# Key-value products in two 64-column halves of the array, and the masks moved to GpSimd

## The chip, the cores and the metric

The kernel runs on one core of one Trainium2 chip. The metric is the device time of one execution in microseconds (us). The profile is of one execution on that core; its span is the time from the first to the last instruction of the program.

The engines are named as the profile names them: PE is TensorE (PEld its weight loads), DVE is VectorE, ACT is ScalarE, POOL is GpSimd, SP is SyncE, which issues most DMAs.

## The reference

The input x has 2048 rows of 512 features. It is normalised per row; the result xn feeds two branches, and the output is x plus both.

```python
def _A_ref(x, wqkv, w_phi, wo):                      # H = 32 heads of 16
    q, k, v = ...                                    # from x @ wqkv
    pq = jnp.einsum("bhsd,hdf->bhsf", q, w_phi)
    pk = jnp.einsum("bhsd,hdf->bhsf", k, w_phi)
    phi_q = concatenate([softmax(pq), softmax(-pq)])
    phi_k = concatenate([softmax(pk), softmax(-pk)])
    kv = jnp.einsum("bhsf,bhsd->bhfd", phi_k, v)
    z  = jnp.einsum("bhsf->bhf", phi_k)
    num = jnp.einsum("bhqf,bhfd->bhqd", phi_q, kv)
    den = jnp.einsum("bhqf,bhf->bhq", phi_q, z) + 1e-6
    return (num / den) @ wo
def _B_ref(x, w1, b1, w2):                           # 512 -> 1792 -> 512
    h = x @ w1 + b1
    return (h * tanh(softplus(h))) @ w2
```

So the first branch is a linear attention: for each of the 32 heads the keys' features (16 from the softmax, 16 from the softmax of the negative) are multiplied with the head's 16 values and summed over all 2048 rows, and the queries' features are then multiplied with that small matrix. Features and values of different heads never meet.

## The kernel before, in words

The 2048 rows are 16 tiles of 128, in 4 groups of 4 tiles. The projection of q and k is folded with w_phi into the weights wqp and wkp.

The first half of the program goes through slots s = 0 to 3 in a loop. In slot s it does, in program order: the exponentials of the keys' logits of group s on ACT (`exponentials`, L228); the products of the features and values of group s - 1 on PE (`accumulate`, L282); two value projections copied by DVE, the logits of the next group and two more value projections copied by ACT (`value`, L164; `logits`, L194; the matmuls are L156); the statistics and normalisation of x two groups ahead (`ln_stats`, and `ln_apply`, L128, on POOL in slots 0 and 1); the division of the features by their sums on DVE (`normalise`, L246 to L259); a number of blocks of the second branch (`hidden`, matmuls L176, activation L183); and the extremes of the next group on DVE (`extremes`, L207 to L218). In slot 2 the transposed q weights are loaded and folded. Each engine runs its instructions in the order in which the program issues them.

After the loop come the exponentials of the first queries, `accumulate(3)`, `mask_kv`, more logits, and then the second half: `attend` (L326) multiplies transposed features of the queries (qT, transposed by DMA that SP issues, L237) with the masked matrix, ACT copies the result out (L335 to L342), `combine` on DVE divides, a DMA transposes (L386), and `project_out` (L408) adds the output projection to the second branch's sum (`second_layer`, L399). `residual` adds x and sends the tile out.

The parts that the change touches:

- `vext` (L81): two buffers with the values of one group, for each tile 4 blocks j of 128 values followed by 8 columns of ones (136 per block). A block holds 8 heads. `value` writes 128 values per block in one copy; the ones are written once at the start by POOL (L443).
- `accumulate(g)`: for each of the 4 blocks, both signs of the softmax (pl) and the 4 tiles of the group, one matmul. Its stationary operand is 128 features (8 heads of 16), its moving operand the 128 values of the same block and one column of ones: 129 columns. It adds up in PSUM over all 16 tiles; `blocks` (L263) gives the place, 432 columns of three banks at a pitch of 144. The result is 128 x 128 for each block, of which only the 8 squares of 16 x 16 on the diagonal mean anything, and a column of sums.
- `mask_kv` (L291): DVE multiplies the 128 x 128 part by a mask with ones in the 8 squares (KVmask, L293 and L297), and spreads the column of sums over 8 columns, masked as well (L303, L308). It writes `kvm`, whose blocks have 144 columns: 128 values, 8 sums, 8 columns of a plain mask.
- `KVmask` and the last 8 columns of `kvm` are written once at the start by three DVE copies (L444 to L446) from `block`, which POOL makes.

Of the kernel before, what the change touches and what calls it, by code (L numbers as in the profile page):

```python
# [8 lines left out]
BF16 = mybir.dt.bfloat16  # L9
# [3 lines left out]
ALU = mybir.AluOpType  # L13
# [4 lines left out]
def kernel(  # L18
# [12 lines left out]
    nc = tc.nc  # L31
    P = 128
    S, D, NH, DH, F = 2048, 512, 32, 16, 1792
    NG = 4
    TPG = 4
# [21 lines left out]
    vpool = ctx.enter_context(tc.tile_pool(name="vpool", bufs=1))  # L57
# [7 lines left out]
    kvm = persist.tile([P, 2, 4, 144], BF16, name="kvm")  # L65
# [12 lines left out]
    mhalf = consts.tile([P, TPG], FP32, name="mhalf")  # L78
    block = consts.tile([P, 8, 16], BF16, name="block")
    KVmask = consts.tile([P, 136], FP32, name="KVmask")  # L80
    vext = [vpool.tile([P, TPG, 4, 136], BF16, name=f"vext{i}") for i in range(2)]  # L81

    ctx.enter_context(tc.manual_schedule())

# [2 lines left out]
    def load_turned(base_col):  # L87

        wT = lnp.tile([P, 4, 512], BF16, name="wT", tag="xn")
        nc.sync.dma_start_transpose(out=wT[:], in_=A_wqkv[:, base_col : base_col + D])  # L90
        return wT

    def fold(wT, dst, dve):

        for kt in range(KT):
            pf = ps.tile([P, 512], FP32, name="pfold", tag="mm")
            for j in range(4):
                nc.tensor.matmul(
                    pf[:, j * P : (j + 1) * P],
                    lhsT=wT[:, j, kt * P : (kt + 1) * P],  # L100
                    rhs=Wbd[:, j, :],
                    start=True,
                    stop=True,
                )
            if kt in dve:
                nc.vector.tensor_copy(dst[:, kt, :], pf[:])
            else:
                nc.scalar.copy(dst[:, kt, :], pf[:])

    def ln_stats(t0, n):  # L110

        stats = lnp.tile([P, TPG, nc.vector.BN_STATS_DIM], FP32, name="stats")
        mv = lnp.tile([P, TPG, nc.vector.BN_AGGR_DIM], FP32, name="mv")
        rstd = lnp.tile([P, TPG], FP32, name="rstd")
        for i in range(n):
            nc.vector.bn_stats(stats[:, i, :], x_sb[:, t0 + i, :])  # L116
        for i in range(n):
            nc.vector.bn_aggr(mv[:, i, :], stats[:, i, :])
        nc.gpsimd.tensor_scalar(
            out=rstd[:, 0:n], in0=mv[:, 0:n, 1], scalar1=1e-5, scalar2=None, op0=ALU.add  # L120
        )
        nc.gpsimd.tensor_tensor(out=rstd[:, 0:n], in0=rstd[:, 0:n], in1=mhalf[:, 0:n], op=ALU.pow)
        return mv, rstd
# [27 lines left out]
    def project(w, t, pp=None):  # L151

        if pp is None:
            pp = ps.tile([P, 512], FP32, name="pproj", tag="mm")[:]
        for kt in range(KT):
            nc.tensor.matmul(  # L156
                pp, lhsT=xnT[:, t, kt, :], rhs=w[:, kt, :],
                start=(kt == 0), stop=(kt == KT - 1),
            )
        return pp  # L160

    def value(t, copy):
        pv = project(wv, t)
        copy(  # L164
            vext[(t // TPG) % 2][:, t % TPG, :, 0:128], pv.rearrange("p (j c) -> p j c", j=4)
        )

    units = iter([(g, f) for g in range(NG) for f in range(FT)])
# [21 lines left out]
    def logits(s, i, copy):  # L190
        if i == 0:
            p_of[s] = smx.tile([P, TPG, 512], BF16, name="p_sb", bufs=1)
        pp = project(wkp if s < NG else wqp, (s % NG) * TPG + i)
        copy(p_of[s][:, i, :], pp)  # L194
# [30 lines left out]
    def exponentials(s, ks=(0, 1)):  # L225
        for k in ks:
            v = e_of[s][:, 2 * k : 2 * k + 2, :, :]
            nc.scalar.activation(v, v, ACT.Exp)  # L228
            if s >= NG:
                turn(s, k)  # L230
# [32 lines left out]
    def blocks(kv, pl, j, width):  # L263

        bank, at = (pl, j) if j < 3 else (2, pl)
        return kv[:, bank, at * 144 : at * 144 + width]

    def by_parts(kv, c0, c1):

        v = kv[:, :, 0:432].rearrange("p b (k c) -> p b k c", c=144)  # L270
        return v[:, 0:2, :, c0:c1], v[:, 2, 0:2, c0:c1]

    kv_of = {}

    def accumulate(g):
        if g == 0:
            kv_of[0] = ps2.tile([P, 3, 512], FP32, name="pkv", tag="kv")
        e = e_of.pop(g)
        for j in range(4):
            for pl in range(2):  # L280
                for i in range(TPG):
                    nc.tensor.matmul(  # L282
                        blocks(kv_of[0], pl, j, 129),
                        lhsT=e[:, i, pl, j * P : (j + 1) * P],
                        rhs=vext[g % 2][:, i, j, 0:129],
                        start=(g == 0 and i == 0 and (j == 0 or (j == 3 and pl == 0))),
                        stop=(g == NG - 1 and i == TPG - 1),
                        skip_group_check=True,
                    )

    def mask_kv():  # L291
        a, b = by_parts(kv_of[0], 0, 128)
        nc.vector.tensor_tensor(  # L293
            out=kvm[:, :, 0:3, 0:128], in0=a,
            in1=KVmask[:, None, None, 0:128].to_broadcast([P, 2, 3, 128]), op=ALU.mult,
        )
        nc.vector.tensor_tensor(  # L297
            out=kvm[:, :, 3, 0:128], in0=b,
            in1=KVmask[:, None, 0:128].to_broadcast([P, 2, 128]), op=ALU.mult,
        )  # L300
        a, b = by_parts(kv_of[0], 128, 129)
        for pl in range(2):
            nc.vector.scalar_tensor_tensor(  # L303
                out=kvm[:, pl, 0:3, 128:136], in0=a[:, pl].to_broadcast([P, 3, 8]), scalar=5e-7,
                in1=KVmask[:, None, 128:136].to_broadcast([P, 3, 8]),
                op0=ALU.add, op1=ALU.mult,
            )
        nc.vector.scalar_tensor_tensor(  # L308
            out=kvm[:, :, 3, 128:136], in0=b.to_broadcast([P, 2, 8]), scalar=5e-7,
            in1=KVmask[:, None, 128:136].to_broadcast([P, 2, 8]), op0=ALU.add, op1=ALU.mult,  # L310
        )

    nd_of, oT_of, po_of, tmp_of = {}, {}, {}, {}
# [121 lines left out]
    for sign in (1, -1):  # L435
        nc.gpsimd.affine_select(
            out=block[:], in_=block[:], pattern=[[-16 * sign, 8], [0, 16]],
# [2 lines left out]
        )  # L440
    nc.gpsimd.memset(mhalf[:], -0.5)
    for i in range(2):
        nc.gpsimd.memset(vext[i][:, :, :, 128:136], 1.0)  # L443
    nc.vector.tensor_copy(KVmask[:, 0:P], block[:].rearrange("p h d -> p (h d)"))  # L444
    nc.vector.tensor_copy(KVmask[:, P : P + 8], block[:, :, 0])
    nc.vector.tensor_copy(  # L446
        kvm[:].rearrange("p l j c -> p (l j) c")[:, :, 136:144],
        block[:, None, :, 0].to_broadcast([P, 8, 8]),
    )


    dve, act = nc.vector.tensor_copy, nc.scalar.copy

    warm = ps.tile([P, 4, P], FP32, name="warm", tag="mm")
    for _ in range(12):
        nc.tensor.matmul(
            warm[:], lhsT=ident[:], rhs=ident[:, None, :].to_broadcast([P, 4, P]),
            start=True, stop=True,
# [4 lines left out]
        out=Wbd[:].rearrange("p j (h e) -> p j h e", h=8),  # L463
        in0=block[:, None, :, :].to_broadcast([P, 4, 8, 16]),
        in1=wsrc[:, :, None, :].to_broadcast([P, 4, 8, 16]),
        op=ALU.mult,
# [17 lines left out]
    def normal(t0, st, xn):  # L484
        ln_apply(t0, TPG, *st, xn, 0)
        for i in (0, 2):
            ln_turn_dma(t0 + i, xn, i)
# [6 lines left out]
    for i in range(TPG):  # L494
        value(i, act)
    hidden(5)

    for s in range(NG):
        exponentials(s, (0, 1) if s else (0,))
        if s > 0:  # L500
            accumulate(s - 1)
        if s < NG:
            for i in range(2 if s else 0):
                value(s * TPG + i, dve)
        if s == 0:
            p_of[1] = smx.tile([P, TPG, 512], BF16, name="p_sb", bufs=1)
            act(p_of[1][:, 0, :], project(wkp, TPG))
            exponentials(0, (1,))
            wide = ps2.tile([P, 3, 512], FP32, name="pwide", tag="kv")
            for i in range(3):  # L510
                project(wkp, TPG + 1 + i, wide[:, i, :])
        else:
            for i in range(TPG):
                logits(s + 1, i, act)
        if 0 < s < NG:
            for i in range(2, TPG):
                value(s * TPG + i, act)
        ln = s + 2 < NG
        if ln:
            t0 = (s + 2) * TPG  # L520
            st = ln_stats(t0, TPG)
            xn = lnp.tile([P, TPG, D], BF16, name="xn", tag="xn")
        elif s == 2:
            wT = load_turned(0)

        normalise(s, 0, (lambda: normal(t0, st, xn)) if ln else None)
        normalise(s, 1)
        if s == 2:
            fold(wT, wqp, ())
        if s == 0:  # L530
            hidden(6)
            act(p_of[1][:, 1:4, :], wide[:])
        hidden((11, 14, 8, 10)[s])
        extremes(s + 1)
# [21 lines left out]
    for h in range(2 * NG):  # L556
        t = 2 * h + 4
# [55 lines left out]
```

## Time and profile before

| what | value |
|---|---|
| median of 3 runs | 183.64 us (183.57 to 183.75) |
| the profiled execution | 183.6 us |
| its span | 181.9 us |
| instructions | 2744 |
| PE matmuls, busy | 1024 records, 175.4 us |
| PE weight loads, busy | 1039 records, 90.2 us |
| DVE, ACT, POOL busy | 146.5, 126.5, 25.0 us |
| granted PE clock | 1.00 |
| DMA | 18.02 MB, 99 GB/s on average |

How to read it: the profiled execution's own time is 1.7 us more than its span, which is what lies around the program. A busy time is the union of an engine's records. Matmul records overlap and their ends are modelled, so the price of a matmul in a stream is the distance between two starts and not the length of a record. In a chain of waits each piece is what the next one waited for; only what lies on it moves the end.

### The profile page before, as it was taken

How to read it: one execution, taken by the hardware profiler on the slowest of the kernel's cores; microseconds unless marked ns; L12 is line 12 of the kernel's file. 1: busy time of each engine (PE TensorE's matmuls, PEld its weight loads, DVE VectorE, ACT ScalarE, POOL GpSimd, SP SyncE). 2: the span in 40 equal slices, each digit the busy share in tenths (PEclk: the TensorE clock that was granted, in tenths of full speed). 3: DMA queues.
4: the chain of work that ended last, by engine and by line, in shares of the span. 5: the costliest groups of instructions: out<-in, count | busy, mean ns of one | idle time of the engine just before them, and what ended most of it. 6: DMA issues, size and time to landing. Idle time of an engine off the chain costs nothing.

```text
span 181.9 us, 2744 instructions
## 1 busy us (share of the span) xinstructions
PE 175.4 (96%) x1024; PEld 90.2 (50%) x1039; DVE 146.5 (81%) x255; ACT 126.5 (70%) x194; POOL 25.0 (14%) x30
## 2 busy tenths in 40 slices
PE   6899999999999999999999999999999999999993
PEld 2454344465444645564465555455554545455561
DVE  2989979986999899988999786399916997647963
ACT  2367999999898899979986989472842558235300
POOL 4403079300793000000000000000000000000000
PEclk9999999999999999999999999999999999999999
DMA  6997796300023600000000840963079302990633
GB/s 145 291 401 267 160 356 175 60 0 5 0 50 65 119 0 0 0 0 4 0 0 0 153 81 10 189 147 63 0 171 203 88 5 41 200 192 31 76 101 115
DMA packets 44393, 18.02 MB, mean 99 GB/s; under 512 B 36828, under 2 KB 43868, under 8 KB 44380
## 3 DMA queue, kind: packets, MB, share of 16 engines
q1 hardware_dynamic: 43408, 17.50, 40.6%
q10 hardware_dynamic: 972, 0.35, 0.7%
q8 instruction: 8, 0.13, 0.3%
q14 instruction: 5, 0.04, 0.1%
HBM read 6.84 MB, written 2.10 MB: 49 GB/s over the span
## 4 chain that ended last, share of the span: by engine, by line
PE 78%; DVE 11%; ACT 4%; DMA 4%; issue 1%; DVEq 0%
PE po L399 22%; PE ph L176 22%; PE pproj L156 17%; PE po L408 7%; PE pkv L282 4%; PE pnd L326 4%; DVE stats L116 4%; ACT e L228 2%; DMA ob<-ob 2%; DMA x_sb<-in_A_x_dram 2%; DVE m L207 2%; DVE xn L128 1%; ACT L183 1%; DVE e L218 1%; DVE wkp L376 1%
## 5 line engine op out<-in xcount | busy, mean ns | idle before, releaser
L399 PE MATMUL po<-w_sb,acts 128*128 128x512 bf16 (+1 forms) x232 | 50.4, 366 | 0.3
L176 PE MATMUL ph<-xnT,w_sb 128*128 128x512 bf16 x224 | 49.5, 379 | 0.4 <-ACT acts L183 0.4
L183 ACT ACTIVATE acts<-ph,b1f 128x512 bf16<-128x512 f32 x56 | 35.2, 703 | 2.8 <-PE ph L176 2.6
L176 PEld LDWEIGHTS <-w_sb 128*128 128x128 bf16 x224 | 21.9, 98 | 26.7 <-issue 0.6
L228 ACT ACTIVATE e<-e 128x2048 bf16<-128x2048 bf16 x16 | 29.8, 1903 | 6.4 <-DVE e L218 6.3
L399 PEld LDWEIGHTS <-acts 128*128 128x128 bf16 x238 | 22.8, 98 | 22.0
L156 PEld LDWEIGHTS <-xnT 128*128 128x128 bf16 x192 | 18.3, 98 | 21.6 <-DMA xnT<-xn 0.8
L194 ACT CAST p_sb<-pproj 128x512 bf16<-128x512 f32 x25 | 13.7, 587 | 9.4 <-PE pproj L156 9.4
L416 DVE TENSOR_TENSOR x_sb<-po,x_sb 128x512 bf16<-128x512 f32 (+1 forms) x17 | 10.6, 655 | 11.4 <-PE po L408 11.4
L246 DVE TENSOR_REDUCE s<-e 128x128 f32<-128x2048 bf16 x8 | 18.2, 2278 | 1.9 <-ACT e L228 1.9
L128 POOL TENSOR_SCALAR xn<-x_sb,mv,rstd 128x512 bf16<-128x512 bf16 x8 | 16.7, 2100 | 0.2
L408 PE MATMUL po<-wqk,ob 128*128 128x512 bf16 (+1 forms) x66 | 14.7, 366 | 0.3 <-DMA ob<-ob 0.2
L156 PE MATMUL pproj<-wv,xnT 128*128 128x512 bf16 x61 | 14.8, 379 | 0.2
L156 PE MATMUL pproj<-wqk,xnT 128*128 128x512 bf16 x62 | 14.4, 379 | 0.1
L335 ACT CAST wkp<-pnd 128x768 bf16<-128x768 f32 x8 | 6.4, 798 | 11.3 <-PE pnd L326 7.4
L207 DVE TENSOR_TENSOR m<-m 128x512 bf16<-128x512 bf16 (+1 forms) x32 | 11.5, 359 | 1.1
L156 PE MATMUL pproj<-wkp,xnT 128*128 128x512 bf16 x50 | 11.8, 379 | 0.1
L207 DVE TENSOR_TENSOR m<-p_sb 128x1024 bf16<-128x1024 bf16 x16 | 11.0, 685 | 1.0 <-ACT p_sb L194 1.0
L326 PEld LDWEIGHTS <-qT 128*128 128x128 bf16 x128 | 9.1, 98 | 3.8
L116 DVE BATCH_NORM_STATS2 stats<-x_sb 128x6 f32<-128x512 bf16 x16 | 10.0, 679 | 1.2 <-DMA x_sb<-in_A_x_dram 1.2
L326 PE MATMUL pnd<-kvm,qT 128*128 128x144 bf16 x128 | 10.6, 226 | 0.0
L259 DVE TENSOR_TENSOR e<-e,r 128x2048 bf16<-128x2048 bf16 x8 | 10.3, 1281 | 0.3
(67 smaller groups left out, 175.2 us busy)
## 6 DMA issues: line engine op xcount, KB each, us to landing
w_sb<-in_B_w_dram SPq DMA_DIRECT2D x2, 1792.0 KB, 8.9
out_dram<-x_sb SPq DMA_DIRECT2D x15, 128.0 KB, 1.9
x_sb<-in_A_x_dram SPq DMA_DIRECT2D x1, 1024.0 KB, 11.7
x_sb<-in_A_x_dram SPq DMA_DIRECT2D x1, 512.0 KB, 4.0
wv<-in_A_wqkv_dram SPq DMA_DIRECT2D x1, 512.0 KB, 4.8
wqk<-in_A_wo_dram SPq DMA_DIRECT2D x1, 512.0 KB
x_sb<-in_A_x_dram SPq DMA_DIRECT2D x1, 256.0 KB, 3.2
x_sb<-in_A_x_dram ACTq DMA_DIRECT2D x1, 256.0 KB, 3.6
```

Source lines behind the costliest of these rows:

```text
L116: nc.vector.bn_stats(stats[:, i, :], x_sb[:, t0 + i, :])
L128: engine.tensor_scalar(out=xn[:, at + i, :], in0=x_sb[:, t0 + i, :], scalar1=mv[:, i, 0:1], scalar2=rstd[:, i : i + 1], op0=ALU.subtract, ...
L156: nc.tensor.matmul(pp, lhsT=xnT[:, t, kt, :], rhs=w[:, kt, :], start=(kt == 0), stop=(kt == KT - 1),)
L176: nc.tensor.matmul(ph[:], lhsT=w1_sb[:, kt, f * P : (f + 1) * P], rhs=xnT[:, g * TPG : (g + 1) * TPG, kt, :], start=(kt == 0), stop=(kt == ...
L183: nc.scalar.activation(acts[:, f, g * 512 : (g + 1) * 512], ph[:], ACT.Mish, bias=b1f[:, f : f + 1])
L194: copy(p_of[s][:, i, :], pp)
L207: nc.vector.tensor_tensor(out=m[:], in0=src[:, :, 0:half], in1=src[:, :, half : 2 * half], op=op)
L228: nc.scalar.activation(v, v, ACT.Exp)
L246: nc.vector.reduce_sum(t[:], v.rearrange("p t l (c e) -> p (t l c) e", e=16), axis=AX.X)
L326: nc.tensor.matmul(blocks(pnd, pl, j, 144), lhsT=qT_of[h][:, i, pl * 4 + j, :], rhs=kvm[:, pl, j, :], start=True, stop=True,)
L399: nc.tensor.matmul(po[:, c], lhsT=acts[:, f, t * P : (t + 1) * P], rhs=w2_sb[:, f, c], start=(f == 0), stop=False,)
L408: nc.tensor.matmul(po[:, c], lhsT=oT_of[h][:, t % 2 * 4 + j, :], rhs=wo_sb[:, j, c], start=False, stop=(j == 3),)
```

## The change

The 128 features of a block are treated as two halves of 64 (4 heads each). `vext` gets, for each half, its own 64 values and 4 columns of ones (68 per half). `accumulate` issues two matmuls where it issued one: half r takes 64 columns of features, the 64 values of the same half and one column of ones, and writes PSUM partitions 64 r to 64 r + 63. `tile_position=(0, 64 * r)` places it in the left or the right 64 columns of the array, with all 128 rows. The squares off the diagonal between the two halves are no longer computed, so `kvm` is filled with zeros once.

`mask_kv` masks each half of the partitions by itself, in two products of 2 x 3 x 64 and 2 x 64 elements per partition. The new function `masks` writes the zeros, `KVmask` and the last columns of `kvm` on POOL; it is called in slot 2 of the loop, behind the load of the transposed weights, and the three DVE copies at the start are gone.

```diff
--- before.py
+++ after.py
@@ -78,7 +78,7 @@
     mhalf = consts.tile([P, TPG], FP32, name="mhalf")
     block = consts.tile([P, 8, 16], BF16, name="block")
     KVmask = consts.tile([P, 136], FP32, name="KVmask")
-    vext = [vpool.tile([P, TPG, 4, 136], BF16, name=f"vext{i}") for i in range(2)]
+    vext = [vpool.tile([P, TPG, 4, 2, 68], BF16, name=f"vext{i}") for i in range(2)]
 
     ctx.enter_context(tc.manual_schedule())
 
@@ -162,7 +162,8 @@
     def value(t, copy):
         pv = project(wv, t)
         copy(
-            vext[(t // TPG) % 2][:, t % TPG, :, 0:128], pv.rearrange("p (j c) -> p j c", j=4)
+            vext[(t // TPG) % 2][:, t % TPG, :, :, 0:64].rearrange("p j r c -> p (j r) c"),
+            pv.rearrange("p (j c) -> p j c", j=8),
         )
 
     units = iter([(g, f) for g in range(NG) for f in range(FT)])
@@ -279,26 +280,31 @@
         for j in range(4):
             for pl in range(2):
                 for i in range(TPG):
-                    nc.tensor.matmul(
-                        blocks(kv_of[0], pl, j, 129),
-                        lhsT=e[:, i, pl, j * P : (j + 1) * P],
-                        rhs=vext[g % 2][:, i, j, 0:129],
-                        start=(g == 0 and i == 0 and (j == 0 or (j == 3 and pl == 0))),
-                        stop=(g == NG - 1 and i == TPG - 1),
-                        skip_group_check=True,
-                    )
+                    for r in range(2):
+                        c = j * P + 64 * r
+                        nc.tensor.matmul(
+                            blocks(kv_of[0], pl, j, 65)[64 * r : 64 * r + 64],
+                            lhsT=e[:, i, pl, c : c + 64],
+                            rhs=vext[g % 2][:, i, j, r, 0:65],
+                            start=(g == 0 and i == 0 and (j == 0 or (j == 3 and pl == 0))),
+                            stop=(g == NG - 1 and i == TPG - 1),
+                            skip_group_check=True,
+                            tile_position=(0, 64 * r),
+                        )
 
     def mask_kv():
-        a, b = by_parts(kv_of[0], 0, 128)
-        nc.vector.tensor_tensor(
-            out=kvm[:, :, 0:3, 0:128], in0=a,
-            in1=KVmask[:, None, None, 0:128].to_broadcast([P, 2, 3, 128]), op=ALU.mult,
-        )
-        nc.vector.tensor_tensor(
-            out=kvm[:, :, 3, 0:128], in0=b,
-            in1=KVmask[:, None, 0:128].to_broadcast([P, 2, 128]), op=ALU.mult,
-        )
-        a, b = by_parts(kv_of[0], 128, 129)
+        for r in range(2):
+            rows, c = slice(64 * r, 64 * r + 64), slice(64 * r, 64 * r + 64)
+            a, b = by_parts(kv_of[0], 0, 64)
+            nc.vector.tensor_tensor(
+                out=kvm[rows, :, 0:3, c], in0=a[rows],
+                in1=KVmask[rows, None, None, c].to_broadcast([64, 2, 3, 64]), op=ALU.mult,
+            )
+            nc.vector.tensor_tensor(
+                out=kvm[rows, :, 3, c], in0=b[rows],
+                in1=KVmask[rows, None, c].to_broadcast([64, 2, 64]), op=ALU.mult,
+            )
+        a, b = by_parts(kv_of[0], 64, 65)
         for pl in range(2):
             nc.vector.scalar_tensor_tensor(
                 out=kvm[:, pl, 0:3, 128:136], in0=a[:, pl].to_broadcast([P, 3, 8]), scalar=5e-7,
@@ -308,6 +314,15 @@
         nc.vector.scalar_tensor_tensor(
             out=kvm[:, :, 3, 128:136], in0=b.to_broadcast([P, 2, 8]), scalar=5e-7,
             in1=KVmask[:, None, 128:136].to_broadcast([P, 2, 8]), op0=ALU.add, op1=ALU.mult,
+        )
+
+    def masks():
+        nc.gpsimd.memset(kvm[:], 0.0)
+        nc.gpsimd.tensor_copy(KVmask[:, 0:P], block[:].rearrange("p h d -> p (h d)"))
+        nc.gpsimd.tensor_copy(KVmask[:, P : P + 8], block[:, :, 0])
+        nc.gpsimd.tensor_copy(
+            kvm[:].rearrange("p l j c -> p (l j) c")[:, :, 136:144],
+            block[:, None, :, 0].to_broadcast([P, 8, 8]),
         )
 
     nd_of, oT_of, po_of, tmp_of = {}, {}, {}, {}
@@ -440,15 +455,7 @@
         )
     nc.gpsimd.memset(mhalf[:], -0.5)
     for i in range(2):
-        nc.gpsimd.memset(vext[i][:, :, :, 128:136], 1.0)
-    nc.vector.tensor_copy(KVmask[:, 0:P], block[:].rearrange("p h d -> p (h d)"))
-    nc.vector.tensor_copy(KVmask[:, P : P + 8], block[:, :, 0])
-    nc.vector.tensor_copy(
-        kvm[:].rearrange("p l j c -> p (l j) c")[:, :, 136:144],
-        block[:, None, :, 0].to_broadcast([P, 8, 8]),
-    )
-
-
+        nc.gpsimd.memset(vext[i][:, :, :, :, 64:68], 1.0)
     dve, act = nc.vector.tensor_copy, nc.scalar.copy
 
     warm = ps.tile([P, 4, P], FP32, name="warm", tag="mm")
@@ -522,6 +529,7 @@
             xn = lnp.tile([P, TPG, D], BF16, name="xn", tag="xn")
         elif s == 2:
             wT = load_turned(0)
+            masks()
 
         normalise(s, 0, (lambda: normal(t0, st, xn)) if ln else None)
         normalise(s, 1)
```

## The prediction

> **What bounds the kernel now.** I read the page first: shares of the engines, then the chain of work that ended last. After that I read that chain in order of time, the groups of instructions by shape, and the table by stretch for the line that the change rewrites.
>
> ```profile
> PE 175.4 (96%) x1024; PEld 90.2 (50%) x1039; DVE 146.5 (81%) x255; ACT 126.5 (70%) x194; POOL 25.0 (14%) x30
> ...
> PE 78%; DVE 11%; ACT 4%; DMA 4%; issue 1%; DVEq 0%
> ```
>
> TensorE (PE) is busy for 96% of the span, and 78% of the chain is PE work. In order of time the chain lies on PE without a break worth naming from 29.07 us to 106.5 us, and again from 115.5 us to 177.9 us. The line that is rewritten, L282 in `accumulate`, runs four times, and each time it is a piece of that chain:
>
> ```profile
> L282 PE MATMUL pkv<-vext,e 128*128 128x129 bf16 x128 | 7.9, 220 | 0.0
> ...
> L282 PEld LDWEIGHTS <-e 128*128 128x128 bf16 x128 | 7.6, 98 | 0.9
> ```
>
> ```profile
> 39.43:41.24 1.81, 1.81 (x32) 1.80 (x31) 1.00 0.03 9
> 60.24:62.05 1.81, 1.81 (x32) 1.80 (x31) 1.00 1.01 194
> 76.76:78.57 1.81, 1.81 (x32) 1.80 (x31) 1.00 0.00 0
> 94.11:95.92 1.81, 1.81 (x32) 1.80 (x31) 1.00 0.00 0
> ```
>
> The second table has, for each stretch, its length, PE busy with L282, its weight loads busy (both in us, with counts) and the clock. The four stretches are 1.81 us each, 7.24 us in all, and nothing waits inside them: a matmul starts every 1.81 / 32 = 56.6 ns. A record's 220 ns is not its price, because the records overlap.
>
> **What TensorE pays per column.** The chain in order of time gives start-to-start times for other widths:
>
> ```profile
> 39.59 1.81 PE pkv L282 x32
> ...
> 69.12 0.89 PE pfold L98 x16
> ...
> 99.54 3.02 PE po L399 x14
> ...
> 104.29 0.50 PE pnd L326 x8
> ```
>
> Columns are start, length, work. 128 columns (L98) take 0.89 / 16 = 55.6 ns, 129 take 56.6, 144 (L326) take 62.5, 512 (L399) take 3.02 / 14 = 215.7. This is a line of (215.7 - 55.6) / 384 = 0.417 ns per column, and 2.2 ns for the instruction. No row here has a width between 14 and 128 columns in a stream.
>
> **The matmuls.** The change takes out 128 matmuls of 129 columns and puts in 256 of 65 columns, alternating between the two column halves of the array. By the line above, a 65-column matmul takes 65 x 0.417 + 2.2 = 29.3 ns. What is unknown is how two neighbours on different halves stand to each other, and no row shows that, so I bound it:
> - Below: both halves run wholly side by side, and a pair costs one pitch, 29.3 ns. 128 x 29.3 = 3.75 us, that is -3.49 us.
> - They take turns: a pair costs 58.6 ns. 128 x 58.6 = 7.50 us, that is +0.26 us.
> - Above: a load and a matmul never come faster than the shortest pitch seen in a stream, 55.6 ns. 256 x 55.6 = 14.23 us, that is +6.99 us. Farther still, each load's record of 98 ns unhidden would make 256 x 98 = 25.1 us, +17.8 us; I keep that outside the range, since the rows show loads of 98 ns following each other every 56 ns.
>
> I take the middle one. The rows nearest to it are the four of L282 themselves: there a stream obeys the column line, one matmul after the other, and the next weight load runs under the present matmul. Nothing in the trace shows two matmuls that share the array.
>
> **The change of mode.** One place of the trace has a weight load that uses part of the array, the 14-row one of the biases:
>
> ```profile
> 8.52 0.38 PE L140 MATMUL ptr<-ident,xn 128*128 128x128 bf16 x4 [0.55 <-DVE wkp L106]
> ...
> 8.83 0.09 PEld L475 LDWEIGHTS <-b1b 14*128 14x128 bf16 x1
> 8.85 0.16 PE L475 MATMUL pb<-ident,b1b 14*128 14x14 bf16 x1
> ...
> 8.95 0.61 PE L156 MATMUL pproj<-wkp,xnT 128*128 128x512 bf16 x2
> ```
>
> Four transposes start at 8.52, so the next instruction was due at 8.52 + 4 x 0.056 = 8.74; it started at 8.85, 0.11 us late. Its 14 columns should take 0.03 us by the rule of 0.417 ns and a generous rest, yet the next matmul starts 0.10 us later, 0.07 us late. Way in and way out cost 0.18 us together. It is one place, on rows and not on columns, and a wait may hide in it; bounds are 0 and, with the in- and outflow of a 512-column matmul (record 379 ns, pitch 216) exposed on both sides, 0.4 us. `accumulate` goes in and out four times: 4 x 0.18 = 0.72 us, between 0 and 1.6.
> The Trainium skill, page "TensorEngine Tiling (Array Packing)", section "Key Properties", says that a change of tiling mode drains TensorE, while a change of tile alone does not. The trace agrees as far as this one place goes: 0.11 us late in, 0.07 us late out. By that rule the four blocks pay the 0.72 us; without it nothing.
>
> **The masks and the ends of the matrix.** DVE loses three small copies at the start (371 + 240 + 131 ns, L444 to L446). They end at 2.80 us, and DVE then waits until 4.00 us for x: nothing is gained.
> GpSimd (POOL) gets a memset of 1152 elements and three small copies, queued behind its last normalisation, which ends at 56.4 us. Its memsets took 205 ns for 128 elements and 103 ns for 4, so 0.83 ns per element: about 1.1 us, and with the copies about 2 us. They are needed by `mask_kv` at 97.8 us, 39 us later, and POOL has nothing else. While POOL ran its long normalisation (48.1 to 56.4 us), one DVE copy took 590 instead of 290 ns and one product 1670 instead of 1230; a repetition would cost DVE up to 0.7 us at about 57 us, which the 0.39 + 0.17 us that DVE waits at 63 us for L164 and the 3.4 us between the last DVE normalisation (56.8) and `accumulate` (60.2) cover. I book 0; uncovered it is at most 0.7.
> `mask_kv` on DVE: 949 + 413 ns for 768 and 256 elements become, per half of the partitions, 384 and 128. The slope is (949 - 413) / 512 = 1.05 ns per element and the rest 145 ns, so 547 + 279 = 826 ns, twice: 1652, which is 290 ns more. DVE is idle for 0.99 us at 102.1 us soon behind it, waiting for an ACT copy, and the first matmul that reads the matrix starts at 104.1 us: nothing on the path.
> The copies of `value` write runs of 64 instead of 128 elements: runs of 128 took 586 ns on ACT beside 587 for unbroken rows, so 0. PE waits for none of them.
>
> **Sum.** 0.26 + 0.72 = +0.98 us on PE, which has no cover: what PE loses in these stretches it loses at the end. The profiled execution took 183.6 us with a span of 181.9, and the median is 183.64, so either base gives the same: 183.6 + 1.0 = **184.6 us**. Within this case, 0 to 1.6 us for the switches give 183.9 to 185.5.
>
> **Rivals.**
> *Side by side* (faster). A pair costs between 29.3 and 42 ns. With 29.3 PE saves 3.49 - 0.72 = 2.77 us. Not all of it arrives. The first `attend` at 104.1 us needs the transposed e, whose DMA was issued at 99.81 and takes 3.3 us: there at 103.1, so 1.0 us of slack. Before that DVE's chain can itself move forward only by what it waits for PE: one block's gain (0.69) at 42.3 us, where it waits 1.96, and 0.56 at 63 us. So 1.0 + 0.69 + 0.56 = 2.25 us arrive: 181.4 us. At 42 ns the saving is 128 x 14.6 = 1.87, less 0.72: 182.5 us. For it: different columns, different PSUM rows, nothing shared by data. Against: no row shows it. It beats the old kernel by more than measurement (0.2%, 0.37 us) when a pair costs under 56.6 - 1.09 / 128, that is 48 ns.
> The same page and section of the Trainium skill state that different tiles can load weights and multiply in parallel; by that rule alone this rival would be the forecast.
> *Loads or issue bind* (slower). If a half's load and matmul need the 55.6 ns of the shortest pitch, PE pays 6.99 + 0.72 = 7.7 us: 191.3 us; at 42 ns per half 128 x (84 - 56.6) = 3.5, and 0.72: 187.8. For it: PE gets 256 more instructions, and the load's record is 98 ns although the pitch is 56.6, so loads are already close behind each other (1.80 busy of 1.81). Against: the load of 128 columns hides wholly today, and the new one is half as wide. It decides from a pair of about 62 ns on.
> The same page, section "Restrictions", says that column tiling switches off the fast weight load. No run here shows what a load without it takes.
> *Nothing to measure.* The pair lands between 48 and 54 ns and pays for the switches: 183.2 to 184.0.
>
> **Chances.** Taking turns 0.37, side by side 0.34, loads or issue 0.22, nothing to measure 0.07. A small part of the first (no cost of switching) falls within 0.2% too. So faster 0.34, same 0.09, slower 0.57; 0.2% is about what a measurement of this kernel can tell. The range reaches to the ends of the rivals, bar the last 0.3 us above: 181.3 to 191.0; beyond it I leave 1 in 10.
>
> **What would show it.** In the profile after, each L282 stretch should be about 2.06 us long instead of 1.81 (1.88 of matmuls and 0.18 of gaps at its ends); 0.94 to 1.5 means side by side, over 2.2 means loads. Starts of neighbours in the stretch should lie 29 ns apart. The transposes of e should not be what PE waits for at `attend`; if they are, the halves overlapped. `mask_kv` should last about 2.2 us (now 1.9), and POOL should finish the masks before 60 us. The forecast is wrong if the pair's pitch is far from 58.6 ns.

## The result and the profile after

The changed kernel takes 182.91 us (median of 6 runs, 182.80 to 183.11) against 183.69 us in the same session: a ratio of 0.9955, 95% interval 0.9942 to 0.9967. It is 0.8 us faster, where I forecast 1.0 us slower. The profiled execution took 182.85 us, its span is 181.1.

First, the line that was rewritten (now L285), in the groups by shape and in the table by stretch. A stretch here begins at the block's first matmul and ends at the start of the next work.

```profile
L285 PE MATMUL pkv<-vext,e 128*64 128x65 bf16 x256 | 4.8, 196 | 0.0
...
L285 PEld LDWEIGHTS <-e 128*64 128x64 bf16 x256 | 4.4, 111 | 1.7 <-DVE m L214 0.8 <-issue 0.8
```

```profile
39.65:40.79 1.14, 1.14 (x64) 1.09 (x64) 1.00 0.00 0
59.88:61.02 1.14, 1.14 (x64) 1.09 (x64) 1.00 2.54 265
76.13:77.26 1.13, 1.13 (x64) 1.08 (x64) 1.00 0.00 0
93.83:94.97 1.14, 1.14 (x64) 1.09 (x64) 1.00 0.00 0
```

64 matmuls now take 1.14 us where 32 took 1.81 (`tile_position` gives each half its own part of the array, called a column tile below). Their starts lie within 1.006 us, 31 steps from pair to pair of 32 ns; inside a pair the starts are 1 to 6 ns apart. So the halves run side by side. Before the block the first start comes 0.09 us later than the last 512-column matmul would have let it, and behind it the next work starts 0.13 us after the last one, where it is 0.03 us behind matmuls of this width on the whole array (an experiment below): the change of mode costs 0.19 us in and out. A block saves 1.81 - 1.14 - 0.09 = 0.58 us, four blocks 2.3 us. Only 0.8 us arrived. The page says who has the chain now:

```profile
PE 173.9 (96%) x1152; PEld 87.0 (48%) x1167; DVE 146.3 (81%) x254; ACT 126.2 (70%) x194; POOL 26.8 (15%) x34
...
PE 50%; DVE 38%; ACT 4%; DMA 4%; issue 2%; POOL 0%; DVEq 0%; POOLq 0%
```

PE's share of the chain fell from 78 to 50%, DVE's rose from 11 to 38%, though the busy times are almost as before. In order of time the chain lies on DVE and ACT from 42.7 to 111.5 us. A few of its pieces (start, length, work):

```profile
62.46 1.92 ACT e L229
64.40 2.30 DVE s L247
...
78.75 1.24 DVE e L219
80.01 1.92 ACT e L229
81.95 2.30 DVE s L247
...
96.30 1.24 DVE e L219
97.56 1.08 ACT e L229
```

That is a loop: the exponentials on ACT (1.94 us until DVE goes on), two normalisations on DVE (64.40 to 74.03, 9.63 us), the extremes of the next group on DVE (5.98 us), and the exponentials again. One turn takes 80.01 - 62.46 = 17.55 us, and no piece of the chain in it is PE's. The same ACT line in the timeline, of the kernel before and then of the changed one (in brackets: idle time before, and what ended it):

```profile
62.76 3.71 ACT L228 ACTIVATE e<-e 128x2048 bf16<-128x2048 bf16 x2 [0.33 <-DVE e L218]
80.32 3.71 ACT L228 ACTIVATE e<-e 128x2048 bf16<-128x2048 bf16 x2 [1.27 <-DVE e L218]
97.88 1.91 ACT L228 ACTIVATE e<-e 128x2048 bf16<-128x2048 bf16 x1 [1.58 <-DVE e L218]
```

```profile
62.46 3.71 ACT L229 ACTIVATE e<-e 128x2048 bf16<-128x2048 bf16 x2 [0.48 <-DVE e L219]
80.01 3.71 ACT L229 ACTIVATE e<-e 128x2048 bf16<-128x2048 bf16 x2 [1.63 <-DVE e L219]
97.56 1.91 ACT L229 ACTIVATE e<-e 128x2048 bf16<-128x2048 bf16 x1 [1.64 <-DVE e L219]
```

The loop had the same period before (17.56 us twice). PE's blocks of L282 lay 16.52 and 17.35 us apart there, so PE gained on the loop, but it had come into these two slots late enough never to stop for it. Now the loop stands 0.31 us earlier, no more: DVE goes on 0.45 us earlier when the first block is through (42.72 us, before 43.17) and loses 0.15 of it at 57 us beside GpSimd's masks. PE, which is earlier than that, stops for the loop. The longest of these stops, on the last value projections of slot 3:

```profile
84.25 1.02 PE L156 MATMUL pproj<-wv,xnT 128*128 128x512 bf16 x4 [0.77 <-ACT p_sb L195]
```

PE waits for a PSUM buffer that ACT empties behind its exponentials. Set side by side, PE's starts tell the whole story in us against before: +0.13 ahead of the first block (scatter of the program's start: the kernel before with one block moved from slot 3 to slot 2, an experiment below, does the same as the one before up to this point and stands at +0.35), -0.45, -1.03 after the first two, then 0.31 given back in slot 2, -1.31 after the third, 0.94 given back in slot 3, -0.95 after the fourth, 0.17 given back at the second matmuls of `attend`, and -0.78 from there on. Saved 2.33 in the four blocks, given back 1.42. In slot 3 PE's lead on the loop had grown by 1.31 - 0.31 = 1.00 us and 0.94 of it was given back, so before the change PE passed there with about 0.06 us to spare.

### The profile page after: what moved, and what is told of

Read it like the earlier page. It is cut to its first block, busy times and chain, and to the rows that moved or that the text cites. A ratio compares the mean times of both kernels' runs of the same rounds, so it can differ in the third digit from the quotient of the medians.

```text
span 181.1 us, 3005 instructions
## 1 busy us (share of the span) xinstructions
PE 173.9 (96%) x1152; PEld 87.0 (48%) x1167; DVE 146.3 (81%) x254; ACT 126.2 (70%) x194; POOL 26.8 (15%) x34
## 4 chain that ended last, share of the span: by engine, by line
PE 50%; DVE 38%; ACT 4%; DMA 4%; issue 2%; POOL 0%; DVEq 0%; POOLq 0%
PE po L414 20%; PE ph L177 8%; DVE s L247 7%; PE po L423 7%; DVE m L208 7%; DVE e L219 5%; PE pproj L156 5%; DVE e L260 4%; ACT e L229 4%; PE pnd L341 3%; DVE r L255 3%; PE warm L463 3%; DVE stats L116 3%; DMA xnT<-xn 2%; DMA ob<-ob 2%
## 5 line engine op out<-in xcount | busy, mean ns | idle before, releaser
L350 ACT CAST wv<-pnd 128x768 bf16<-128x768 f32 x8 | 6.3, 792 | 5.9 <-PE pnd L341 3.7
```

## The experiments

The theory was that the loop of DVE and ACT binds now and eats what PE saves. The rival: the change's own extra work eats it, namely a longer `mask_kv` on DVE and GpSimd's masks in DVE's way.

**Less work in the loop, in both kernels.** The last product of the second normalisation is left out in slots 0 to 3, so half of the keys' features stay undivided.

```diff
+        if k == 1:
+            return
         nc.vector.tensor_tensor(
             out=vv, in0=vv, in1=r2[:, :, None, :].to_broadcast([P, 128, 8, 2]), op=ALU.mult
         )
```

> The kernel before, with one DVE product of 1.23 us left out per slot (the last product of the second normalisation in slots 0 to 3, so half of the keys' features stay undivided). Theory (DVE and ACT form a loop of 17.55 us per slot that was hidden just behind PE before the change and binds after it): PE binds here, so 183.4 to 183.7 us, no more than 0.3 below the kernel before. Rival (the loop binds in neither kernel; the change's saving is eaten by its own longer mask_kv and by GpSimd's masks): also about 183.6. This run is the base for the next one.

> The changed kernel with the same product left out. Theory (the DVE and ACT loop binds): with the loop 1.23 us shorter per slot PE's whole saving of 4 x 0.58 = 2.3 us arrives, about 181.3 us (181.0 to 181.7), and PE's stalls in slots 2 and 3 are gone. Rival (own extra work eats it): about 182.6 to 182.9, as the changed kernel itself, since mask_kv and the masks are unchanged.

Measured: the kernel before 183.78 us, ratio 1.0002 (0.9992 to 1.0012); the changed kernel 181.29 us, ratio 0.9867 (0.9852 to 0.9882). The same 1.23 us per slot are worth nothing in one kernel and 1.6 us in the other, and with them the change is worth 183.78 - 181.29 = 2.5 us: PE's whole saving of 2.3, within the scatter. The page of the changed kernel with less DVE work shows the chain back on PE:

```profile
PE 81%; DVE 9%; ACT 4%; DMA 2%; issue 2%; POOL 0%; DVEq 0%; POOLq 0%
```

`mask_kv` and the masks are in this kernel as well. By itself that doesn't exclude the rival, for a lighter DVE could hide the extra work too; the sizes do: of the 1.5 us that didn't arrive, the masks explain 0.15 (below), and DVE idles for 0.65 us behind `mask_kv`.

**The order of the matmuls.** Two kernels change only the order within a block: four matmuls on one half, then four on the other; and all 32 on the left, then all 32 on the right.

```diff
-                for i in range(TPG):
-                    for r in range(2):
+                for r in range(2):
+                    for i in range(TPG):
```

```diff
-        for j in range(4):
-            for pl in range(2):
-                for i in range(TPG):
-                    for r in range(2):
+        for r in range(2):
+            for j in range(4):
+                for pl in range(2):
+                    for i in range(TPG):
```

> The changed kernel with four matmuls in a row on one half of the array and then four on the other, in place of alternating. If two matmuls overlap only when neighbours in the queue are on different halves, a block of 64 takes about 64 x 29.3 = 1.88 us plus switches (2.1 us), and the time goes back to about 183.7. If TensorE looks ahead far enough to fill both halves, the block stays at 1.0 us and the time at 182.9.

> The changed kernel with all 32 matmuls of a block on the left half first and then the 32 on the right. With runs of four the block came to 1.034 us beside 1.006 alternating, so TensorE looked ahead over at least four loads and matmuls. If its look-ahead covers 32 of each, the block stays near 1.05 us; if not, the halves run one after the other, 64 x about 31 ns = 2.0 us, and the time goes to about 183.7 to 184.

In runs of four a block takes 0.03 us longer than alternating, in runs of 32 nearly twice as long; the first stretch of each, from its first matmul to the next work:

```profile
39.63:40.79 1.16, 1.16 (x64) 1.12 (x64) 1.00 0.00 0
```

```profile
39.83:41.88 2.05, 2.05 (x64) 2.00 (x64) 1.00 0.04 8
```

The times are 182.87 and 185.24 us, one run each. TensorE finds the matmul for the idle half behind four others, but not behind 32. So what is said above, that each engine runs its instructions in the order of the program, does not hold for PE's matmuls on different halves: in strict order each of the 16 runs of four needs at least three steps of 30.9 ns (the next experiment's pitch), 1.48 us in all as an estimate, and the 64 starts took 1.03. The second trace shows about where the sight ends: in each of its blocks only three pairs of starts, around the change of half, lie 1 to 8 ns apart, so the right half was found when three matmuls of the left were still waiting (the records don't name the half; this is read from the starts). The second kernel is also my forecast come true: halves in turn, 1.92 us from the first start to the last (I had 1.88), 0.19 us for the switches as above, and more time than before.

**Halves without column tiles.** Weights of 128 features, moving operand of 65 columns, the two halves side by side in PSUM.

```diff
-                            blocks(kv_of[0], pl, j, 65)[64 * r : 64 * r + 64],
-                            lhsT=e[:, i, pl, c : c + 64],
+                            blocks(kv_of[0], pl, j, 130)[:, 65 * r : 65 * r + 65],
+                            lhsT=e[:, i, pl, j * P : (j + 1) * P],
...
-                            tile_position=(0, 64 * r),
...
-            a, b = by_parts(kv_of[0], 0, 64)
+            a, b = by_parts(kv_of[0], 65 * r, 65 * r + 64)
```

> The changed kernel without tile positions: each half's 64 values and column of ones go through the whole array with all 128 features as weights, side by side in PSUM, and mask_kv reads the half that it needs. 256 matmuls of 65 columns with loads of 128 columns, no change of mode. By the column line of the forecast 29.3 ns each: 64 x 29.3 = 1.88 us per block, no gaps at its ends, about 183.7 to 184.0 us. If a load or an issue takes longer than 29.3 ns, the pitch shows it: at 55.6 ns 3.6 us per block and about 190 us.

```profile
40.07:42.05 1.98, 1.98 (x64) 1.98 (x63) 1.00 0.03 8
```

1.98 / 64 = 30.9 ns per matmul and no gap on the way in. The time is 184.81 us, one run, with everything else of the change in place. So narrower matmuls alone lose; what gains is that two share the array. My column line (29.3 ns) was 1.6 ns low.

**Four tiles of 32.** 512 matmuls of 33 columns; `vext` in runs of 32 and 4 ones, `mask_kv` in quarters.

```diff
-                            lhsT=e[:, i, pl, c : c + 64],
-                            rhs=vext[g % 2][:, i, j, r, 0:65],
+                            lhsT=e[:, i, pl, c : c + 32],
+                            rhs=vext[g % 2][:, i, j, r, 0:33],
...
-                            tile_position=(0, 64 * r),
+                            tile_position=(0, 32 * r),
```

> The changed kernel with four column tiles of 32: 32 features by their 32 values and a column of ones, 512 matmuls of 33 columns, mask_kv in four quarters of the partitions. If the tiles run side by side and nothing else limits, four matmuls take one pitch of 33 columns, about 16 ns, and a block 32 x 16 = 0.5 us and 0.2 us of switches. If each load with its matmul has a least time, a block shows it: the halves came to 1.006 us for 64, that is 15.7 ns each, so at that floor 128 take 2.0 us. The time is not expected to fall even in the first case (182.8 to 183.3), since the loop of DVE and ACT binds and mask_kv gets 0.6 us longer; in the second about 183.5 to 184.

```profile
39.81:40.94 1.13, 1.13 (x128) 1.10 (x128) 1.00 0.00 0
```

128 matmuls in the same 1.13 us, so 8 ns each and 32 ns for four on average. Neither of my two numbers came: there is no least time of 15.7 ns per matmul, and 33 columns don't come down to the 16 ns of the column line. The average hides two paces, the same in all four blocks: matmuls 9 to 32 come at 25 ns for four, and later ones at about 33 ns for four (24 starts in each 0.2 us). So 32 ns is no least time of a tile; what slows the later ones, the loads and the issue of so many instructions included, isn't shown. The time, 183.05 us in one run, doesn't fall, as expected.

**Moving PE's work into its stall.** One block of the second branch from slot 3 to slot 2, in both kernels.

```diff
-        hidden((11, 14, 8, 10)[s])
+        hidden((11, 14, 9, 9)[s])
```

> The changed kernel with one block of the second branch (0.86 us of TensorE) moved from slot 3 to slot 2, nothing else. TensorE stalls 0.27 us in slot 2 and 0.72 us in slot 3, waiting for PSUM that ACT frees late because its exponentials wait for DVE. Theory (the loop of DVE and ACT binds in these slots, TensorE arrives early): the block fills the stall of slot 3, and the time falls by 0.5 to 0.8 us to 182.1 to 182.4. Rival (the saving is lost to the change's own extra work on DVE and POOL): nothing moves, 182.8 to 183.0.

> The kernel before with the same block moved from slot 3 to slot 2. Theory: TensorE has no stall there to fill, so the time stays at 183.6 to 183.9. If the new place were better by itself, whatever the change, this kernel gains too (183.0 to 183.3).

A miss: 182.92 us, ratio 0.9959 (0.9946 to 0.9971), no faster than the change alone; before, 183.82 us, ratio 1.0007 (0.9997 to 1.0017). The stall in slot 3 did go (0.77 to 0.07 us), and PE was 0.85 us earlier behind it. It then waits at `attend`; the two pieces in the timeline of PE, of the changed kernel and then of this one:

```profile
103.18 0.66 PE L341 MATMUL pnd<-kvm,qT 128*128 128x144 bf16 x8
...
105.57 0.66 PE L341 MATMUL pnd<-kvm,qT 128*128 128x144 bf16 x8
```

```profile
102.74 0.67 PE L341 MATMUL pnd<-kvm,qT 128*128 128x144 bf16 x8 [0.25 <-DMA qT<-e]
...
105.59 0.66 PE L341 MATMUL pnd<-kvm,qT 128*128 128x144 bf16 x8 [0.45 <-ACT ds L357]
```

Exponentials of the queries start at 97.56 us in the one and 97.58 in the other, for the loop sets them, and the second `attend` starts at 105.57 and 105.59. The wait only moved. The time alone is the one that the rival forecast; what speaks for the theory is the trace, in which PE comes 0.85 us earlier and the loop and the second `attend` stay where they were. I had taken the stall for the cost, and it was only where the cost showed.

**The masks at the start.** `masks()` is called before the first matmuls and no longer in slot 2.

```diff
+    masks()
     dve, act = nc.vector.tensor_copy, nc.scalar.copy
...
             wT = load_turned(0)
-            masks()
```

> The changed kernel with GpSimd's masks at the start of the program (its idle time from 2.7 to 5.4 us) and not in slot 2. In slot 2 two DVE products took 0.91 us beside GpSimd's copies and not 0.75, and DVE's lead fell from 0.45 to 0.30 us. If that delay lies on the loop that binds, the time falls by 0.15 us to about 182.75. If it is covered, it stays at 182.9.

182.81 us, ratio 0.9946 (0.9934 to 0.9958), whose interval overlaps that of the change, so the times show no gain. The trace shows the delay itself, on DVE's products beside GpSimd's copies in the changed kernel, and without them:

```profile
56.96 0.91 DVE L208 TENSOR_TENSOR m<-m 128x512 bf16<-128x512 bf16 x2
```

```profile
56.81 0.75 DVE L208 TENSOR_TENSOR m<-m 128x512 bf16<-128x512 bf16 x2
```

The delay lies on the loop. Without it the exponentials start 0.30 us earlier than in the changed kernel (62.15, 79.71 and 97.27 us), and so does the second `attend` (105.28 against 105.57). Of this 0.15 us is there before the first block (39.50 against 39.65), where the masks of slot 2 have no part; the other 0.15 comes at 57 us, where they were.

**A shorter loop with nothing left out.** The softmax sums as a tree of additions.

```diff
-        nc.vector.reduce_sum(
-            t[:], v.rearrange("p t l (c e) -> p (t l c) e", e=16), axis=AX.X
-        )
+        src = v.rearrange("p t l (c e) -> p (t l c) e", e=16)
+        with nc.allow_low_precision("the softmaxes are bf16"):
+            for half in (8, 4, 2):
+                m = smx.tile([P, 128, half], BF16, name=f"m{half}", bufs=1)
+                nc.vector.tensor_tensor(
+                    out=m[:], in0=src[:, :, 0:half], in1=src[:, :, half : 2 * half], op=ALU.add
+                )
+                src = m[:]
+        nc.vector.tensor_tensor(out=t[:], in0=src[:, :, 0], in1=src[:, :, 1], op=ALU.add)
```

> The changed kernel with the sums of the softmaxes taken as a tree of four additions in bf16, in place of one reduction of 2.28 us: by the rows of the extremes 685 + 425 + 292 + about 220 ns and three gaps of 30, 1.7 us. DVE's part of the loop gets 0.55 us shorter per normalisation, 1.1 us per slot. Theory (the loop of DVE and ACT binds): TensorE's saving arrives, 181.2 to 181.8 us. Rival (the change's own extra work eats it): 182.9.

> The kernel before with the same tree. Theory: TensorE binds and DVE's saving is worth nothing, 183.5 to 183.8 us. If the tree helps by itself, this kernel falls as far as the changed one, and the difference between the two stays at 0.8 us.

> The changed kernel with the tree and with GpSimd's masks at the start. If DVE binds no more, the 0.15 us that GpSimd costs it in slot 2 are covered and this is as fast as the tree alone, within 0.1 us.

The changed kernel with the tree takes 181.47 us, ratio 0.9868 (0.9851 to 0.9884), the fastest version with the whole computation; the kernel before with the tree 183.84 us, ratio 0.9999 (0.9989 to 1.0009); with the masks at the start as well 181.61 us, ratio 0.9874 (0.9858 to 0.9891), the same. The loop with the tree, in ACT's timeline:

```profile
62.21 3.71 ACT L229 ACTIVATE e<-e 128x2048 bf16<-128x2048 bf16 x2
78.80 3.71 ACT L229 ACTIVATE e<-e 128x2048 bf16<-128x2048 bf16 x2 [0.55 <-DVE e L219]
95.38 3.71 ACT L229 ACTIVATE e<-e 128x2048 bf16<-128x2048 bf16 x2 [0.46 <-DVE e L219]
```

16.6 us per turn, and the chain is on PE again (78%, DVE 9%). Neither edit is worth its price alone: the tree nothing, the tiles 0.8 us, both together 2.4.

## Why the prediction was wrong

- **The matmuls, the step that failed.** I took the middle of three cases, halves that take turns at 58.6 ns a pair, because nothing in the trace showed two matmuls sharing the array. They share it: 32 ns a pair. That nothing shows a thing was no evidence against it, since no instruction of the kernel before could have shown it; I gave it 0.34 and the forecast 0.37, a difference that no row carried. The bound from below (29.3 ns) was nearly the truth. On PE the sum was thus -2.33 us and not +0.98.
The Trainium skill, page "TensorEngine Tiling (Array Packing)", section "Key Properties", had it right that different tiles load and multiply in parallel; here 32 ns a pair beside 30.9 ns for one matmul of the same width alone.
- **The change of mode.** Forecast 0.18 us per block, from one place with a 14-row load; measured 0.19. Right in its sum, and partly by luck: the place was a part of the rows and not of the columns, and the parts differ (0.11 in and 0.07 out forecast, 0.09 and 0.10 measured). The upper bound of 0.4 was generous: 379 - 216 ns on both sides is 0.33.
- **What arrives of a saving.** For the rival "side by side" I let 2.25 us arrive; 0.8 did. I let DVE come forward by its wait for PE, 0.56 us at 63 us. But the reduction behind that wait, at 64.70 us, was due at the same time by ACT's exponentials, which had started when DVE's own extremes ended: take PE's wait away, and ACT's takes its place. In the changed kernel it stands there, 0.75 us before the reduction. A gap shows the release that came last, not the next one behind it. The reduction in the kernel before and then in the changed one:

```profile
64.70 2.29 DVE L246 TENSOR_REDUCE s<-e 128x128 f32<-128x2048 bf16 x1
```

```profile
64.40 2.29 DVE L247 TENSOR_REDUCE s<-e 128x128 f32<-128x2048 bf16 x1 [0.75 <-ACT e L229]
```

- **The slack at `attend`.** The DMA of the transposed features did not decide; the second `attend` did, which waits until ACT has emptied the one PSUM buffer of the first. I hadn't looked at that wait.
- **The masks on GpSimd.** Booked 0 with 0.56 us of cover; the cover was the one that doesn't exist, and in the 3.4 us up to `accumulate` DVE wasn't idle but at its extremes. They cost DVE 0.16 us, and in the traces 0.15 of it stands on the loop and at the second `attend`; in the times it is too small to show.
- **`mask_kv`, the copies at the start, the copies of `value`.** Right. `mask_kv`'s records add up to 2.19 us (forecast 2.2, before 1.87); it runs from 97.45 to 99.34 us, DVE still idles 0.65 us behind it, and without the three copies at the start DVE only waits longer for x (3.77 us in place of 2.37 and 1.20).
- **Loads or issue bind.** Excluded for the halves: 128 loads and matmuls fit into 1.13 us with four tiles, where the change has 64. The argument that half a load is half as long was wrong, though: its record is longer, 111 ns.

## What to carry to other kernels

In these runs a matmul on half of the array cost the time of one on the whole array only where no matmul for the other half was near in the queue; alternate the halves, in runs of four at most. Before pricing a saving on the busiest engine, look for the next loop of other engines and measure its period: where it comes close to the engine's own, a saving on the engine alone arrives only until the loop binds, and both have to get shorter for the rest. And a stall that is filled proves nothing until the end moves.

## What the runs showed of the hardware

- Column tiles of 64 or 32 columns ran side by side: 32 ns for two matmuls of 65 columns, and 32 ns on average for four of 33.
- With a load for each, matmuls of 65 columns followed each other every 30.9 ns on the whole array. Four tiles with 33 columns took one matmul each in 25 ns at first (matmuls 9 to 32 of a block) and in 33 ns later; why is open.
- A load of 64 columns had a longer record (111 ns) than one of 128 (97 to 98 ns), at a pitch of 32 ns for a pair of 65 columns against 30.9 for one with the longer load.
- Going into column tiles cost 0.09 us with either width, and out of them about 0.10 us.
- Matmuls for the other half were found behind three that waited (runs of four, and the change of half in runs of 32), not behind more.
- Two DVE products of 128x512 took 0.91 us beside GpSimd's copies and 0.75 us without them.
